# A gated linear attention followed by a multiplicative FFN: alpha of chunks 2 to 7 loaded by pairs of chunks

## The chip, the core and the metric

The kernel runs on one core of one Trainium2 chip. The metric is the device time of one execution in microseconds, smaller is better. Several executions are made of each kernel, and their median counts. One execution is taken with the hardware profiler; its span is the time between the first and the last instruction of the program, and its device time is a little longer.

## What is computed

The first part is a recurrence over 768 positions, for 4 batches and 8 heads of 48 values. Its output, read as 3,072 tokens of 384 values, goes through a feed-forward part with two gates that are multiplied.

```python
for t in range(S):
    state = alpha[:, :, t, :, None] * state + np.einsum('bhd,bhe->bhde', k[:, :, t], v[:, :, t])
    y[:, :, t] = np.einsum('bhd,bhde->bhe', q[:, :, t], state)
...
x = y.transpose(0, 2, 1, 3).reshape(B * S, H * D)
a = x @ w1
b = x @ w2
h = a * b @ w3
return h @ w_out
```

The shapes: q, k, v and alpha are 4 x 8 x 768 x 48 in float32, with alpha between 0.8 and 1; w1 and w2 are 384 x 1,024, w3 is 1,024 x 1,024, w_out is 1,024 x 384, all in float64. In DRAM the 48 values of one head at one position are 192 contiguous bytes, and the next position of the same head follows directly.

## The kernel before

**Chunks.** The positions are cut into N = 24 chunks of C = 128, six for each batch. A chunk's positions lie on the 128 partitions, its 8 heads of 48 values beside one another, 384 columns. For chunk n, `load_a` (L132) fetches alpha, `load_kq` (L138, L139) k and q, and `load_v` (L144) v. Each of these is one transfer of 192 KB in 1,024 rows of 192 bytes. All go through SP's queue, except v of chunks 3 to 7, which goes through POOL's.

**Decays.** `logs` (L272) takes the logarithm of alpha on ACT. `decays` (L287) multiplies it on TensorE with a 128 x 128 matrix of zeros and ones, `sums`, which adds up the logarithms along the positions: for even chunks with a minus sign and over the positions that come after, for odd ones over those up to and including the position itself. So two neighbouring chunks meet in a common point, between them. The exponentials of the sum and of its negative are `e` (L293, L294), and VectorE multiplies k and q with them (`decayed`, L303). Chunks below LATE = 10 do the sum as one float32 product; later ones split the logarithm in two float32r parts and do two products (L290).

**Attention in a chunk.** TensorE transposes k and q (`transposed`, L325) and ACT copies the result out (L327). `scores` (L365) multiplies keys and queries, VectorE masks (L368), `attend_state` (L385) applies the state from before, `attend` (L391) adds the chunk's own part, ACT copies it out (L395), and a store by SP (L262) writes it to `xd` in DRAM. `outer` (L337) makes the chunk's own contribution to the state, and VectorE adds it (L345, L347). At each even chunk but the first of a batch, `advance` (L354 to L356) on POOL scales the state with a decay. That decay is the product of three rows: two of exponentials (L296, L298) and the row of alpha at the chunk's first position (L279). They are written to a small tensor `ends` in DRAM by POOL's queue, and read back in another layout (L311).

**Buffers.** Alpha has three buffers (tag "ac"), k and q three, the logarithm two, v five. A transfer into a buffer waits until its last reader is done, so the load of alpha of chunk 5 waits for the logarithm of chunk 2 and for the small transfer L279 that reads chunk 2's alpha.

**Weights.** Beside the chunks, `convert` turns the float64 weights, loaded as 64-bit integers (L192, 512 KB each), into float32 by bit operations on VectorE and ACT (L200 to L210), and splits them into float32r parts (L217, L219, and by way of TensorE L233 to L235).

**Order.** The main loop, L600 to L671, runs over the chunks. In each turn n it issues the stores, alpha of chunk n + 5, k and q of n + 3 (from chunk 6 on n + 4), attention of chunks n - 1 and n, transposes of n + 1, weight conversion, the product of n + 2 with its decays, logarithms of n + 4 and sums of n + 3. Before the loop a prologue loads alpha of chunks 0 to 4. A scheduler then orders the instructions of each engine by its own estimate of when they can run; `issue_after` gives it a limit for single ones. In turn 5 `split_x` (L413 to L415) splits the first 384 tokens of x into three parts in the buffer "x3" of pool `tr[0]`, and the first gates' products begin (L421), which fill the rest of the kernel.

Of the kernel before, what the change touches and what calls it, by code (L numbers as in the profile page):

```python
# [10 lines left out]
FP32 = mybir.dt.float32  # L11
FP32R = mybir.dt.float32r
# [3 lines left out]
AF = mybir.ActivationFunctionType  # L16
# [32 lines left out]
def kernel(  # L49
# [12 lines left out]
    nc = tc.nc  # L62
    B, H, S, D = q.shape
    C = 128
    DM = H * D
    DF = moe_w1.shape[1]
    NCH = S // C
    N = B * NCH
    NP = H // 2
    DP = 64  # L70
    KM = DM // C
# [3 lines left out]
    TG = G * C  # L75
    CW = 512
    AHEAD = 4
    LATE = 10
    assert D <= DP and DM % C == 0 and DF % CW == 0 and S % C == 0 and N % G == 0
    assert DM <= 512 and TG <= 512  # L80

    def pool(name, bufs, stack=ctx, **kw):
        return stack.enter_context(tc.tile_pool(name=name, bufs=bufs, **kw))
# [4 lines left out]
    tr = [pool("tr0", 1)]  # L88
# [14 lines left out]
    def bank():  # L103
        return ps.tile([C, 512], FP32, tag="bank", name="bank")

    st, mark = {}, {}
# [10 lines left out]
    ends = {n: dram.tile([3, DM], FP32, name=f"ends{n}") for n in range(2, N, 2) if n % NCH}  # L117
# [7 lines left out]
    def rows(src, n):  # L125
        b, c = divmod(n, NCH)
        return src[b, :, ds(c * C, C), :].rearrange("h p d -> p h d")

    def load_a(n):
        if n < N:  # L130
            st["a", n] = inp.tile([C, H, D], FP32, tag="ac", name="ac")
            nc.sync.dma_start(out=st["a", n], in_=rows(alpha, n))  # L132

# [7 lines left out]
    def load_v(n):  # L141
        if n < N:
            st["v", n] = vs[n % len(vs)]
            (nc.gpsimd if 2 < n < 8 else nc.sync).dma_start(out=st["v", n][:, :, 0:D], in_=rows(v, n))  # L144

    nc.scalar.preload_act_table_set(LN_EXP_SET)
    load_a(0)
    load_kq(0)
    load_a(1)
    load_v(0)  # L150
    load_kq(1)
    load_a(2)


# [26 lines left out]
    make_identity(nc, ident)  # L181
    nc.gpsimd.tensor_copy(out=signs[:, 0], in_=ident)
    nc.gpsimd.tensor_scalar_mul(signs[:, 1], ident, -1.0)
    for x in Ts + decs:
        nc.gpsimd.memset(x, 0.0)

# [80 lines left out]
    def logs(n):  # L267
        if n >= N:
            return
        a = st.pop(("a", n)).rearrange("p h d -> p (h d)")  # L270
        la = st["la", n] = work.tile([C, DM], FP32, tag="la", name="la")
        nc.scalar.activation(la, a, AF.Ln)  # L272
        if n >= LATE:

            t = st["la", n] = work.tile([C, 2, DM], FP32R, tag="la2", name="la2", bufs=1)
            nc.scalar.copy(t[:, 0], la)
            nc.vector.tensor_sub(t[:, 1], la, t[:, 0].bitcast(FP32))
        if n in ends:
            nc.gpsimd.dma_start(out=ends[n][2:3], in_=a[0:1])  # L279

    def decays(n):
        if n >= N:
            return
        lc = bank()[:, 0:DM]
        la = st.pop(("la", n))
        if n < LATE:
            nc.tensor.matmul(lc, sums[:, n % 2].bitcast(FP32), la, start=True, stop=True)  # L287
        else:
            for i in range(2):
                nc.tensor.matmul(lc, sums[:, n % 2], la[:, i], start=(i == 0), stop=(i == 1))  # L290

        e = st["e", n] = work.tile([C, 2, DM], FP32, tag="e", name="e", bufs=3)
        nc.scalar.activation(e[:, 0], lc, AF.Exp, scale=-1.0)  # L293
        mark["e", n] = nc.scalar.activation(e[:, 1], lc, AF.Exp).ins  # L294
        if n in ends:
            mark["pool"] = nc.gpsimd.dma_start(out=ends[n][0:1], in_=e[0:1, 0]).ins  # L296
        if n + 1 in ends:
            mark["pool"] = nc.gpsimd.dma_start(out=ends[n + 1][1:2], in_=e[C - 1:C, 1]).ins  # L298
        load_ends(n)
# [6 lines left out]
    def load_ends(n):  # L306
        if n not in ends:
            return
        with nc.allow_non_contiguous_dma(reason="single values to partitions"):
            for i in range(2):  # L310
                nc.gpsimd.dma_start(out=decs[n // 2 % 2][ds(DP * i, D)].rearrange("d m j -> d (m j)"),  # L311
                                    in_=ends[n].rearrange("m (j i d) -> i d (m j)", i=2, d=D)[i])
# [95 lines left out]

    def split_x(g, i):
        x = st.pop(("xT", g))  # L410
        t = tr[i].tile([C, 3, KM, TG], FP32R, tag="x3", name="x3")
        st["x3", g] = t
        nc.scalar.activation(t[:, 0], x, AF.Copy, scale=1.0 - 2.0 ** -13)  # L413
        nc.vector.tensor_sub(t[:, 1], x, t[:, 0].bitcast(FP32))
        mark["x3"] = nc.vector.scalar_tensor_tensor(t[:, 2], t[:, 0].bitcast(FP32), -1.0 - 1.0 / P, x,  # L415
                                                    op0=ALU.mult, op1=ALU.add).ins
# [146 lines left out]
    fill = deque()  # L563
# [12 lines left out]
    for half in range(DF // CW):  # L576
        for kk in range(KM):
            weights.extend(load_gates(i, kk, half) for i in range(2))

    logs(0)  # L580
    decays(0)
    decayed(0)
    transposed(0)
    with after_marks(("e", 0)):
        logs(1)
    decays(1)
    fetch(1)
    load_a(3)
    load_kq(2)
    decayed(1)  # L590
    fetch(2)
    load_v(1)
    load_a(4)

# [5 lines left out]
    for n in range(N + 1):  # L600
# [5 lines left out]
        for m in (n + 3,) * (n <= FIRST) + (n + 4,) * (n >= FIRST):  # L606
            load_kq(m)
            if n < FIRST - 2:
                fetch(raws)
            if n >= FIRST:  # L610
                load_v(m - 1)
# [8 lines left out]
        if n - 2 in begin and n > FIRST:  # L620
            g, tiles = begin[n - 2]
            with after_marks(("ms", n), ("qkT", n + 1)):
                split_x(g, 0)
            fill.extend(gate(g, f) for f in tiles)
        pieces = (3, 3, 2, 0)[(n - FIRST) % 4] if n >= FIRST else 0
        if n == 0:
            with after_marks(("qkT", 0)):
                logs(2)
            decays(2)
            with after_marks(("e", 2)):  # L630
                logs(3)
# [29 lines left out]
        if n == FIRST - 1:  # L661
            assert len(done) == 2 * KM
            g, tiles = begin[n - 2]
            with after_marks("l"):
                split_x(g, 0)
            fill.extend(gate(g, f) for f in tiles)
# [32 lines left out]
    for i, x in enumerate(todo):  # L699
        with tc.issue_after(ends_of_part1[0]), tc.issue_after(ends_of_part1[1]):  # L700
            while order and i >= order[0][0]:
                split_x(*order.pop(0)[2:])
                if order:
                    load_x(order[0][2], nc.gpsimd)
        for _ in x:
            pass
        owed += 2.0
        with tc.issue_after(ends_of_part1[0]), tc.issue_after(ends_of_part1[1]):
            convert(int(owed), 4)
        owed -= int(owed)  # L710
        if i == halfway + 1:
            first.close()
            w3o = pool("w3op", 1, side="right", reuse_waits="tile").tile([C, 3, KF, DM], FP32R, name="w3o")
        if folded < KF:
            if w3o and folds and next(folds[0], None) is None:
                folds.popleft()
                folded += 1
        elif lastp is None:
            settle()
            folding.close()  # L720
            lastp = pool("lastp", 1, reuse_waits="tile")
            for n in range(4):
                load_ab(n)
# [40 lines left out]
```

## Time and profile before

| | |
|---|---|
| median of three runs | 477.14 us (476.88 to 477.63) |
| the profiled execution | 476.57 us |
| its span | 474.8 us |
| TensorE busy over the span | 456.5 us, 96% |
| VectorE, ACT, POOL busy | 359.1, 279.6, 76.6 us |
| alpha's loads (L132) | 24 transfers of 192 KB, median 5.2 us from issue to landing |
| logarithms (L272) | 24 of 546 ns |
| packets under 512 bytes | 99,360 of 148,783 |

How to read it: lines such as L287 are lines of the kernel before. A busy time counts an engine's instructions, not what it waits for. The rows over 40 slices of the span have one digit per slice of 11.87 us, the busy share in tenths. The chain of waits follows the work that ended last back to the start: at each step to what released it. Float32 products appear as two records each.

### The profile page before, as it was taken

The numbers are of one execution on the slowest core, as the hardware profiler recorded it, in microseconds if no ns is written. First come the engines' busy times: TensorE is split into PE (matmuls) and PEld (weight loads), VectorE is DVE, ScalarE is ACT, GpSimd is POOL, SyncE is SP. The second block draws the span as 40 slices with busy tenths as digits, with TensorE's granted clock in tenths as the row PEclk, the third lists the DMA queues.
The fourth block names the chain that finished last, engine by engine and source line by source line (L and its number), as shares of the span: only waits on it lengthen the run. The fifth ranks groups of instructions, "written<-read, shape, count | busy, mean of one in ns | idle before, by whom it ended". The sixth has DMA issues, their size and how long they took to land.

```text
span 474.8 us, 10017 instructions
## 1 busy us (share of the span) xinstructions
PE 456.5 (96%) x3836; PEld 432.7 (91%) x3836; DVE 359.1 (76%) x578; ACT 279.6 (59%) x555; POOL 76.6 (16%) x144
## 2 busy tenths in 40 slices
PE   4878899999999999999999999999999999999997
PEld 2666689899999998999999999999999999999996
DVE  2778796899979888999999868855542876666761
ACT  4668765768668563988877675654543533333330
POOL 3433122104201310121221202111011000000000
PEclk9988899999999999999999999999999999999999
DMA  9999999999899944467685532202012976555511
GB/s 179 216 209 189 228 187 247 221 239 224 184 221 206 240 142 136 137 207 251 204 271 164 182 128 84 99 35 101 33 51 88 257 233 191 163 166 174 177 51 50
DMA packets 148783, 80.29 MB, mean 169 GB/s; under 512 B 99360, under 2 KB 140576, under 8 KB 148736
## 3 DMA queue, kind: packets, MB, share of 16 engines
q1 hardware_dynamic: 142960, 64.44, 55.5%
q0 software_dynamic: 5776, 15.22, 10.2%
q8 instruction: 30, 0.49, 0.5%
q14 instruction: 17, 0.14, 0.1%
HBM read 57.58 MB, written 22.06 MB: 168 GB/s over the span
## 4 chain that ended last, share of the span: by engine, by line
PE 85%; DMA 5%; DVE 4%; ACT 2%; issue 1%; SPq 1%; POOL 1%; DVEq 0%; ACTq 0%; POOLq 0%
PE bank L421 70%; PE bank L365 4%; DMA kq<-in_q_dram 4%; PE bank L391 3%; PE bank L325 2%; PE bank L385 2%; PE bank L523 1%; PE bank L337 1%; PE bank L287 1%; DMA xT<-xd 1%; PE bank L290 1%; DVE qk L303 1%; DVE ms L368 1%; DVE x L415 1%; SPq L262 1%
## 5 line engine op out<-in xcount | busy, mean ns | idle before, releaser
L421 PE MATMUL bank<-x,w 128*128 128x384 f32 x1152 | 212.6, 338 | 1.1 <-DVE x L415 0.6
L421 PEld LDWEIGHTS bank<-x,w 128*128 128x128 f32 x1152 | 200.2, 188 | 4.0 <-PE bank L421 0.9
L421 PE MATMUL bank<-w3o,ab 128*128 128x384 f32 x576 | 100.2, 336 | 0.0
L421 PEld LDWEIGHTS bank<-w3o,ab 128*128 128x128 f32 x576 | 99.9, 188 | 0.0
L446 ACT ACTIVATE bank<-bank 128x384 f32<-128x384 f32 x96 | 45.7, 476 | 41.2 <-PE bank L421 40.6
L430 ACT ACTIVATE t<-bank 128x384 f32<-128x384 f32 x64 | 31.5, 494 | 57.4 <-PE bank L421 56.2
L496 POOL DMA_DIRECT2D abd<-ab x45 | 26.3, 583 | 144.9 <-DVE ab L482 126.2
L482 DVE TENSOR_TENSOR ab<-bank,r 128x384 f32<-128x384 f32 x44 | 24.4, 554 | 24.9 <-ACT bank L446 15.9
L552 DVE TENSOR_TENSOR ab<-abl,ab 128x1024 fp32r<-128x1024 f32 x24 | 29.4, 1224 | 12.3 <-ACT ab L551 12.3
L327 ACT COPY qkT<-bank 128x512 f32<-128x512 f32 x48 | 25.8, 590 | 20.5 <-PE bank L325 20.5
L551 ACT ACTIVATE ab<-abl 128x1024 fp32r<-128x1024 f32 x24 | 25.4, 1060 | 20.2 <-PE bank L421 18.3
L421 PE MATMUL bank<-wo,w3T 128*128 128x384 f32 x192 | 35.9, 334 | 0.0
L303 DVE TENSOR_TENSOR qk<-kq,e 128x768 f32<-128x768 f32 x24 | 22.9, 954 | 14.9 <-ACT e L294 8.3
L421 PEld LDWEIGHTS bank<-wo,w3T 128*128 128x128 f32 x192 | 33.5, 188 | 0.0
L368 DVE TENSOR_TENSOR ms<-bank,keep 128x512 int32<-128x512 int32 x48 | 31.2, 683 | 0.1
L432 DVE SCALAR_TENSOR_TENSOR o<-bank,t 128x384 f32<-128x384 f32 x24 | 13.4, 557 | 23.0 <-issue 13.7
L432 DVE SCALAR_TENSOR_TENSOR r<-bank,t 128x384 f32<-128x384 f32 x40 | 22.1, 554 | 11.4 <-ACT t L430 8.5
L205 ACT ACTIVATE power<-power,rebias 128x512 uint32<-128x512 uint32 (+1 forms) x36 | 25.1, 699 | 9.2 <-DVE power L204 9.0
L365 PEld LDWEIGHTS bank<-qkT 48*128 48x128 f32 x384 | 24.4, 193 | 6.3 <-issue 3.0
L365 PE MATMUL bank<-qkT 48*128 48x128 f32 x384 | 29.3, 291 | 0.4 <-ACT x L395 0.4
L553 DVE SCALAR_TENSOR_TENSOR ab<-ab,abl 128x1024 fp32r<-128x1024 f32 x24 | 29.2, 1218 | 0.0
L391 PE MATMUL bank<-ms,v 128*64 128x128 f32 x384 | 27.6, 289 | 0.0
(81 smaller groups left out, 578.9 us busy)
## 6 DMA issues: line engine op xcount, KB each, us to landing
raw<-in_moe_w_dram SPq DMA_DIRECT2D x28, 512.0 KB, 5.2
abl<-abd SPq DMA_DIRECT2D x24, 512.0 KB, 4.4
abd<-ab POOLq DMA_DIRECT2D x45, 192.0 KB, 2.8
xT<-xd POOLq DMA_DIRECT2D x9, 576.0 KB, 4.5
ac<-in_alpha_dram SPq DMA_DIRECT2D x24, 192.0 KB, 5.2
kq<-in_k_dram SPq DMA_DIRECT2D x24, 192.0 KB, 5.7
kq<-in_q_dram SPq DMA_DIRECT2D x24, 192.0 KB, 5.7
xd<-x SPq DMA_DIRECT2D x48, 96.0 KB, 4.0
```

The costliest lines, as they stand in the source:

```text
L303: mark["qk", n] = nc.vector.tensor_mul(qks[n % 3][:, :, :, 0:D], st.pop(("kq", n)), st.pop(("e", n)).rearrange("p i (h d) -> p i h d", h=H ...
L327: mark["qkT", n] = nc.scalar.copy(qkT[:, :, :, ds(DP * half, DP)], tp[half]).ins
L365: nc.tensor.matmul(sc[i][:, j, :], qkT[r, 0, j, :], qkT[r, 1, j, :], start=True, stop=True)
L368: masked = nc.vector.tensor_tensor(ms[:, i].bitcast(I32), sc[i].bitcast(I32), keep_bc, op=ALU.bitwise_and)
L391: nc.tensor.matmul(to, vc[:, 2 * j + i, :], ms[:, i, j, :], start=(n % NCH == 0 and j % HP == 0), stop=(j % HP == HP - 1), skip_group_chec ...
L421: nc.tensor.matmul(p, w[part][i], x[part][i], start=start and part == parts[0] and i == 0, stop=stop and part == parts[-1] and i == n - 1, ...
L430: nc.scalar.activation(t, p1, AF.Copy, scale=(1.0 + 1.0 / P) * scale)
L432: nc.vector.scalar_tensor_tensor(to, p2, scale, t, op0=ALU.mult, op1=ALU.add)
L446: nc.scalar.activation(p, p, AF.Copy, scale=1.0 + 1.0 / P)
L496: (nc.gpsimd if late else nc.sync).dma_start(out=abd[g][:, f, :], in_=ab)
L552: nc.vector.tensor_sub(t[:, 1], ab, t[:, 0].bitcast(FP32))
L553: nc.vector.scalar_tensor_tensor(t[:, 2], t[:, 0].bitcast(FP32), -1.0 - 1.0 / P, ab, op0=ALU.mult, op1=ALU.add)
```

## The change

Alpha of chunks 2 to 7 is loaded as three pairs, (2, 3), (4, 5) and (6, 7). A pair's 256 positions go onto 128 partitions by twos: partition p holds positions 2p and 2p + 1, for each head 96 values that are contiguous in DRAM, 384 bytes. The first chunk of a pair thus lies on partitions 0 to 63 and the second on 64 to 127. One logarithm over 768 columns, in place, serves a pair. The sums of a chunk become two float32 products that accumulate, one with the even positions of the pair and one with the odd ones, each with a matrix that takes the chunk's positions from its half of the partitions and puts the sums out in order (`sums2`, four 128 x 128 matrices, made on POOL at the start). The pairs and the matrices lie in the memory of the first "x3" buffer, which is free until the first `split_x`; there are two buffers for three pairs, so the pair (6, 7) takes the place of (2, 3). The rows of alpha for `ends` of chunks 2 and 4 are copied from DRAM to DRAM instead of out of the loaded tile. The prologue loads the pair (2, 3) where it loaded chunk 2 and the pair (4, 5) where it loaded chunk 4; turn 1 of the loop loads (6, 7) where it loaded chunk 6; the loads of chunks 3, 5 and 7 fall away.

```diff
+    PAIRED = 8
...
+    def paired(n):
+        return 2 <= n < PAIRED
+
     def load_a(n):
-        if n < N:
+        if paired(n):
+            if n % 2 == 0:
+                b, c = divmod(n, NCH)
+                x = pairs[n // 2 % 2]
+                nc.sync.dma_start(out=x.rearrange("p h s d -> p h (s d)"), in_=alpha[b, :, ds(c * C, 2 * C), :].rearrange("h (p s) d -> p h (s d)", s=2))
+                st["a", n] = st["a", n + 1] = x
+        elif n < N:
             st["a", n] = inp.tile([C, H, D], FP32, tag="ac", name="ac")
             nc.sync.dma_start(out=st["a", n], in_=rows(alpha, n))
...
+    spare = tr[0].tile([C, 3 * KM * TG], FP32R, tag="x3", name="x3")[:].bitcast(FP32)
+    sums2 = spare[:, 0:4 * C].rearrange("p (e s t) -> p e s t", e=2, s=2)
+    pairs = [spare[:, ds(4 * C + i * 2 * DM, 2 * DM)].rearrange("p (h s d) -> p h s d", h=H, s=2) for i in range(2)]
...
+    for e, val in ((0, -1.0), (1, 1.0)):
+        nc.gpsimd.memset(sums2[ds(e * C // 2, C // 2), e], val)
+        nc.gpsimd.memset(sums2[ds((1 - e) * C // 2, C // 2), e], 0.0)
+        nc.gpsimd.affine_select(out=sums2[:, e], in_=sums2[:, e], fill=0.0, base=e * C,
+                                compare_op=mybir.AluOpType.is_ge if e else mybir.AluOpType.is_gt,
+                                pattern=[[-1, 2], [1, C]] if e else [[1, 2], [-1, C]],
+                                channel_multiplier=-2 if e else 2)
     for x in Ts + decs:
         nc.gpsimd.memset(x, 0.0)
...
     def logs(n):
         if n >= N:
             return
-        a = st.pop(("a", n)).rearrange("p h d -> p (h d)")
+        a = st.pop(("a", n))
+        if paired(n):
+            if n % 2 == 0:
+                nc.scalar.activation(a, a, AF.Ln)
+                st["la", n] = st["la", n + 1] = a
+                b, c = divmod(n, NCH)
+                if n in ends:
+                    nc.gpsimd.dma_start(out=ends[n][2:3].rearrange("m (h d) -> m h d", h=H), in_=alpha[b:b + 1, :, c * C, :])
+            return
+        a = a.rearrange("p h d -> p (h d)")
...
         la = st.pop(("la", n))
-        if n < LATE:
+        if paired(n):
+            for i in range(2):
+                nc.tensor.matmul(lc.rearrange("p (h d) -> p h d", h=H), sums2[:, n % 2, i], la[:, :, i, :],
+                                 start=(i == 0), stop=(i == 1))
+        elif n < LATE:
             nc.tensor.matmul(lc, sums[:, n % 2].bitcast(FP32), la, start=True, stop=True)
...
     def split_x(g, i):
         x = st.pop(("xT", g))
-        t = tr[i].tile([C, 3, KM, TG], FP32R, tag="x3", name="x3")
+        t = tr[i].tile([C, 3 * KM * TG], FP32R, tag="x3", name="x3").rearrange("p (s k t) -> p s k t", s=3, k=KM)
```

## The prediction

> **What bounds the kernel now.** I read the page's forty slices first, to see where TensorE is not the limit.
>
> ```profile
> PE   4878899999999999999999999999999999999997
> PEclk9988899999999999999999999999999999999999
> DMA  9999999999899944467685532202012976555511
> ```
>
> One slice is 11.87 us. From slice six on TensorE is full, and the stretches answer from 60.45 to 474 us gives 410.49 busy of 413.55. The change touches chunks 2 to 7, all in the first five slices, so its worth is the shift of the moment at which TensorE becomes full. Before that the DMA engines are full too. So I read the chain of waits for the first 60 us.
>
> ```profile
> 13.68 1.35 PE bank L287 x2
> ...
> 18.17 4.77 DMA kq<-in_q_dram
> ...
> 24.91 6.25 DMA kq<-in_q_dram
> ...
> 47.43 6.22 DMA kq<-in_q_dram
> ...
> 59.03 1.28 DVE x L415
> 60.31 0.14 issue
> 60.45 2.34 PE bank L421 x12
> ```
>
> The columns are start, length, what. Three loads of q carry 17 us of it: up to 31.16 us the chain is loads that arrive one after the other; from 31.16 to 45 it runs through DVE and ACT (weight conversion, masks, exponentials); then the load for chunk 7 and the split of x. How much room TensorE has there, the stretches answer shows (busy us of PE, PEld, DVE, ACT, POOL; granted clock; DMA share; GB/s):
>
> ```profile
> 12.56:47.71 35.15, 28.88 (x390) 22.15 (x389) 27.90 (x49) 24.95 (x54) 12.96 (x22) 0.90 1.11 205
> 31.00:39.00 8.00, 6.81 (x60) 5.54 (x56) 7.45 (x14) 4.96 (x12) 2.48 (x4) 0.57 1.02 189
> 2.00:7.60 5.60, 1.62 (x2) 0.50 (x2) 1.25 (x3) 1.94 (x5) 2.23 (x10) 1.00 1.33 196
> ```
>
> TensorE idles 35.15 - 28.88 = 6.27 us between the transposes of chunks 1 and 6 (L325 at 12.56 and 47.71). These idle times are its waits for loads and for what follows from them; VectorE waits 6.5 us in five multiplications (L303) for q:
>
> ```profile
> PE bank L325 <- DVE qk L303: 3.7, 3, 1.9
> PE bank L325 <- DVE T L347: 1.2, 1, 1.2
> PE bank L337 <- DMA v<-in_v_dram: 0.9, 1, 0.9
> PE bank L287 <- ACT la L272: 0.8, 1, 0.8
> DVE qk L303 <- DMA kq<-in_q_dram: 6.5, 5, 2.2
> ```
>
> [...] From 2.00 to 7.60 us the trace holds 192-byte packets alone, 5,809 of them: 5.60 us x 16 / 5,809 = 15.4 ns. [...] The trace has a clock of 0.57 from 31 to 39 us, after the idle stretch before 32.53, and an L287 product takes 1.35 us at 13.68 but 0.65 at 62.78.
>
> **The change part by part.**
>
> *Alpha's loads.* Six loads of 192 KB in 1,024 rows of 192 B become three of 384 KB in 1,024 rows of 384 B. One old load takes 64 packets per engine x 15.4 ns = 0.99 us. For 384 B no row of the trace stands. Bounds: if bytes set the price, nothing is saved; if packets do, 0.49 us per chunk, 3.0 in all. [...] I take that estimate: 0.29 us per chunk, 1.7 in all.
>
> *What moves on SP's queue.* SP issues in order[...]. Before, L132 for chunks 4 and 5 sits from 13.78 for 3.50 us, as chunk 5's buffer waits until the small transfer out of chunk 2's (L279, issued at 11.53) has landed; k and q of chunk 3 stand behind it, and the DMA moves only 113 GB/s from 21 to 22 us, some 0.5 us lost. In the changed order chunk 3's alpha comes with 2, 5 with 4, 7 with 6; the pairs have own buffers, that wait is gone. The new wait: the load of 6 and 7 needs the buffer of 2 and 3, free after chunk 3's sums on TensorE; k, q and the raw weights queue behind it. I expect these sums done by 17.4 us (below) and the load at about 20, so it costs nothing. Beyond 18.5 to 20 it would. q of chunk 3 then lands at 22.94 - 4 x 0.29 - 0.5 = 21.3, q of chunk 4, with chunk 7's alpha 0.70 earlier in the line, at 31.16 - 1.7 - 0.5 + 0.7 = 29.6: about 1.5 us early.
>
> *The sums.* Each of six chunks gets a second fp32 product: 0.65 us at full clock, 1.3 at half. Chunk 2's starts at 13.6, where the half clock ends after one product: +0.65; chunks 3, 4, 5 and 7 +0.65 each; chunk 6's (38.18) falls at the edge of the half clock, +1.0. Sum 4.25 us, bounds 3.9 and 7.8. It has 6.27 us of idle to lie in, so at most 2.0 us of earlier arrival can be used by this engine. Step by step: chunk 2's +0.65 is given back where chunk 3 no longer waits 0.77 for its logarithm (16.40): chunk 3's sums end at 17.4, scores (L365) of chunk 1 start at 17.4 against 17.24. Chunk 4's lies before the wait of 1.12 at 24.14. Chunk 5's lies before L385, which waited already for POOL's state (L356, done 28.50), then L325 of chunk 4 waited 1.19 at 32.53. That state comes from chunk 2's exponential, 0.65 later, so at 29.1; L385 and L365 then end at 30.9 instead of 32.53: this agrees with 29.6 for q plus 0.96 for L303. So 1.5 us is won at 31. From 32.53 to 45.83 TensorE has no gap: chunk 6's and 7's +1.65 leave it at 45.98 instead of 45.83 even with the 1.5, still ahead of 47.71 - 1.5 by 0.2 us. There the cover ends: TensorE is late next. The strided moving operand (runs of 48 in 96) has no row; I take nothing for it; the upper bound, a doubled read in all twelve products, would be 7.8 us more.
>
> *Logarithms.* Six of 0.54 become three over 768 columns. From L272 (0.55 for 384) and L413 (1.17 for 1,152) 0.81 ns per column, so 0.86: ACT saves 0.66 us. The first now needs 384 KB landed: about 0.4 later than 11.40, ended at 12.8, before chunk 2's sums at 13.6. The pair 4, 5 ends at 20.5 against 20.32; w L217 and qkT L327 queue behind, 0.2 us, hidden before L325's wait at 24.14. At 40.28 chunk 7's logarithm leaves the chain: -0.41. But the exponential ahead of it waits for chunk 6's sums: 39.18 - 1.5 + 1.0 = 38.7 instead of 39.38. With the logarithm gone, w L217 starts at 39.6 instead of 40.55. So of 1.5 us about 1.0 is left, and VectorE (L219, L368), ACT L395, the store, the load for chunk 7 and the split of x follow it to 60.45.
>
> *POOL.* Four memsets (0.28 each, as L185) and two selections over 256 columns (0.28 for 128, so 0.5): 2.1 us after 3.6, ending at 6.4; POOL was idle from 4.22 to 11.53. The first product waits for sums (L173), issued ahead of them, so not for these. Rows 0 of alpha go from DRAM to DRAM: waits of 7.30 and 3.67 us go, but the next (L311, 20.64) still waits for the exponential's row to land. Nothing won. The split of x takes the pairs' memory over: it waits for chunk 7's sums, 44 us, against its 55.22: free.
>
> Sum: the profiled execution took 476.57 us (span 474.8); -1.0 makes 475.6. The three runs have a median of 477.14, 0.57 above it; on that scale 476.1.
>
> **The rivals.**
>
> *TensorE takes the bound* (slower). Place: 12.56 to 47.71. If the half clock holds over most of the added products, they cost 7.8 us against 6.27 idle: +1.5, and no load is used; with gaps that cannot be used, up to +2.5. It decides from about 5.3 us of added time. For it: 28.88 busy of 35.15, no gap from 32.53 on, and a half clock twice. Against: most gaps lie just behind the new products. 478.9.
>
> *The longer rows save nothing* (it doesn't do what it says): bytes set the price. Chunk 7's alpha still comes earlier, 0.99 at q of chunk 4, less 0.5 of SP's gap, and TensorE's added products give back nothing: +0.5, 477.6. [...]
>
> *Fuller TensorE, full clock.* With fewer gaps the clock may not fall at 31 us; half clock there lasted about 6.9 us, 3.4 us of work. VectorE (27.90 busy) is late next: -2.5, 474.6. Against: before 31 its gaps stay.
>
> **How the numbers follow.** No change is within 0.2%, 0.95 us, about what a measurement of this kernel can tell. Forecast 0.50, own range -2.2 to -0.3 (474.9 to 476.8): faster 0.35, same 0.15. TensorE 0.22, all slower. No saving 0.17: 0.10 same, 0.07 slower. Full clock 0.11, faster. Together 0.46, 0.25, 0.29. For 8 in 10 the range goes from 474.6, the full clock's value, to 479.0, most of TensorE's case.
>
> **What would show it.** Right: q of chunks 3 and 4 landing near 21.3 and 29.6, L303's waits for q under 5 us, SP without its 3.5 us stand, TensorE's idle from the first to the second of those transposes near 1 to 2 us, L421's run of twelve starting near 59.5. Wrong: a rate in alpha's loads as before; TensorE waiting less and still starting that run at 60.5 or later; SP standing at the load of 6 and 7; more time at half clock.

## The result, and the profile after

| | before | after |
|---|---|---|
| median | 477.26 us (20 runs, 476.09 to 478.86) | 475.75 us (20 runs, 473.91 to 478.06) |
| ratio | | 0.9967, 95% interval 0.9955 to 0.9980 |
| the profiled execution | 476.57 us | 475.50 us |
| its span | 474.8 us | 473.8 us |
| mean granted clock of TensorE | 0.989 | 0.996 |
| packets under 512 bytes | 99,360 | 96,240 |

The changed kernel is 1.5 us faster, a third of a per cent; the forecast was 1.0 us. The same three rows of the page's forty slices, for the kernel after:

```profile
PE   4988899999999999999999999999999999999996
PEclk9999999999999999999999999999999999999999
DMA  9999999999999934567685532212013986555511
```

The second row has lost its three eights: each of these slices now has 90% of the full clock or more. The stretches of the kernel after (busy us of PE, PEld, DVE, ACT, POOL with their instructions; granted clock; DMA share; GB/s) show it more finely; those of the kernel before that the prediction does not show come first:

```profile
48.00:57.00 9.00, 8.27 (x115) 6.10 (x111) 6.62 (x12) 6.86 (x14) 0.66 (x2) 0.81 1.17 249
57.00:61.00 4.00, 2.83 (x11) 1.86 (x12) 4.00 (x6) 3.22 (x8) 1.92 (x3) 1.00 0.73 179
```

and of the kernel after:

```profile
12.50:31.00 18.50, 17.72 (x220) 12.23 (x220) 14.86 (x28) 12.83 (x28) 5.78 (x11) 1.00 1.16 228
31.00:39.00 8.00, 7.09 (x107) 5.40 (x104) 6.93 (x12) 6.44 (x15) 3.15 (x5) 1.00 1.10 246
39.00:48.00 9.00, 7.85 (x120) 5.96 (x116) 6.40 (x12) 5.54 (x13) 3.47 (x7) 1.00 0.94 203
48.00:57.00 9.00, 7.68 (x93) 5.15 (x89) 8.22 (x13) 8.04 (x19) 2.33 (x4) 1.00 0.91 213
57.00:61.00 4.00, 3.62 (x11) 3.14 (x12) 2.55 (x5) 2.08 (x6) 0.07 (x1) 0.57 1.02 210
```

From 31 to 39 us the DMA now moves 246 GB/s against 189, and TensorE runs at 1.00 against 0.57; its 7.09 us of busy time hold 107 matmul records where 6.81 us held 60. From 48 to 57 us it is 1.00 against 0.81. The half clock has not vanished, though. It stands at the end of the table, 0.57 over the 4 us in which the first gates begin, with 0.50 in every part of them between 57.5 and 60.5 us; the kernel before had 1.00 there.

VectorE's waits in the first 62 us of the kernel after (us in total, times, longest):

```profile
DVE qk L337 <- ACT e L328: 8.1, 2, 4.4
DVE w L240 <- ACT w L238: 3.7, 6, 0.7
DVE qk L337 <- DMA kq<-in_q_dram: 1.6, 2, 1.2
```

L337 is the multiplication that was L303. It waits 1.6 us for q where it waited 6.5; the split of a weight (L240, before L219) in turn waits 3.7 us for ACT where it waited 1.5. From 12.5 to 57 us VectorE is busy for 36.41 us, against 34.81 before: 1.6 us more of its work is done. The loads of q land at these times (us), each the start of its issue on SP plus the time to its landing:

| q of chunk | before | after |
|---|---|---|
| 3 | 22.94 | 21.77 |
| 4 | 31.16 | 30.92 |
| 5 | 38.80 | 36.51 |
| 6 | 46.51 | 44.11 |
| 7 | 53.65 | 48.28 |

For chunk 4 these are the lines on the two loads, issued at 24.91 before and at 24.20 after:

```profile
DMA to landing us min/median/max: 6.3/6.3/6.3
DMA to landing us min/median/max: 6.7/6.7/6.7
```

All five come earlier, but that of chunk 4 by 0.24 us alone. The chain of waits of the kernel after (start, length, what):

```profile
24.20 5.21 DMA kq<-in_q_dram
29.41 0.51 POOL T L390
29.98 0.24 issue
30.22 0.68 DVE mant L228
30.97 0.45 issue
31.42 0.95 DVE qk L337
32.37 0.61 DVE mant L231
...
55.99 1.28 DVE x L448
57.31 1.30 PE bank L455 x3
58.67 3.32 PE bank L455 x12
61.99 0.32 PE bank L321
```

The chain breaks the load of q of chunk 4 off at 29.41, which is not its landing: its sixteen parts report from 29.12 to 30.92, VectorE needs all of them, and POOL's scaling of the state (L390) does not use q. What VectorE does meanwhile differs. Before, it had nothing left and stood 2.13 us until q was there; the addition of POOL's state and the conversion came behind the multiplication. After, it waits 0.67 us for POOL's state, which comes later (29.41 to 29.92, before 27.99 to 28.50), does the addition and two instructions of weight conversion, and comes to the multiplication at 31.42, 0.17 later than before. But that other work is now out of the way. The next split of a weight (L240) runs at 33.67 against 35.10, with one mask fewer ahead of it; where both kernels have done the same work, ahead of the next L222 (L201 before), it is 35.48 against 36.31, 0.83 us. Then q of chunk 5 has landed 2.29 us earlier: its L337 starts at 36.60 against 38.89. The split of x (L448) starts at 55.99 in the chain, against 57.76.

The last two lines take part of that back: the twelve products start at 58.67 against 60.45, and last 3.32 us, with a granted clock of 0.68 over them, against 2.34. The sums behind them start at 61.99 against 62.78: 0.8 us of the 1.8 is left. The spans differ by 1.0.

### The profile page after: what moved, and what is told of

Same layout as the page of the kernel before. It is cut to its first block, busy times and chain, and to the rows that moved or that the text cites. A ratio compares the mean times of both kernels' runs of the same rounds, so it can differ in the third digit from the quotient of the medians.

```text
span 473.8 us, 10043 instructions
## 1 busy us (share of the span) xinstructions
PE 458.9 (97%) x3848; PEld 433.5 (92%) x3848; DVE 359.0 (76%) x578; ACT 279.4 (59%) x552; POOL 79.8 (17%) x150
## 2 busy tenths in 40 slices
DMA packets 145663, 80.29 MB, mean 169 GB/s; under 512 B 96240, under 2 KB 137456, under 8 KB 145616
## 4 chain that ended last, share of the span: by engine, by line
PE 87%; DMA 4%; DVE 3%; SPq 3%; issue 1%; ACT 1%; POOL 0%; DVEq 0%
PE bank L455 72%; PE bank L399 4%; PE bank L425 4%; DMA kq<-in_q_dram 3%; PE bank L419 2%; PE bank L359 2%; PE bank L557 1%; DMA x<-in_alpha_dram 1%; PE bank L371 1%; PE bank L324 1%; SPq L213 1%; DVE ms L402 1%; SPq L149 1%; DVE qk L337 1%; SPq L148 1%
## 5 line engine op out<-in xcount | busy, mean ns | idle before, releaser
L361 ACT COPY qkT<-bank 128x512 f32<-128x512 f32 x48 | 25.8, 589 | 21.3 <-PE bank L359 21.3
L585 ACT ACTIVATE ab<-abl 128x1024 fp32r<-128x1024 f32 x24 | 25.5, 1061 | 21.3 <-PE bank L455 18.0
L337 DVE TENSOR_TENSOR qk<-kq,e 128x768 f32<-128x768 f32 x24 | 22.9, 953 | 10.2 <-ACT e L328 8.3
L425 PE MATMUL bank<-ms,v 128*64 128x128 f32 x384 | 26.3, 279 | 0.0
```

The lines of the kernel that those rows point to most:

```text
L337: mark["qk", n] = nc.vector.tensor_mul(qks[n % 3][:, :, :, 0:D], st.pop(("kq", n)), st.pop(("e", n)).rearrange("p i (h d) -> p i h d", h=H ...
L361: mark["qkT", n] = nc.scalar.copy(qkT[:, :, :, ds(DP * half, DP)], tp[half]).ins
L425: nc.tensor.matmul(to, vc[:, 2 * j + i, :], ms[:, i, j, :], start=(n % NCH == 0 and j % HP == 0), stop=(j % HP == HP - 1), skip_group_chec ...
```

## The experiments

Every ratio is to the kernel before, run on the same chip, and comes from medians. The profiled execution of a kernel can lie over 2 us from its median, so the profiles are read for places, the ratios for sizes. One thing can be read from all profiles alike: the start of the last product of the sums (166 to 171 us; 173 and 176 with extra loads), and the time from there to the end of the span. That remainder is 307.2 to 307.5 us in before, after and every experiment but the last. So whatever these executions win or lose, they do before that point.

### Rows of 192 bytes in the changed kernel

Only the transfers change: a pair comes by two of them, in the old rows.

```diff
-                nc.sync.dma_start(out=x.rearrange("p h s d -> p h (s d)"), in_=alpha[b, :, ds(c * C, 2 * C), :].rearrange("h (p s) d -> p h (s d)", s=2))
+                for i in range(2):
+                    nc.sync.dma_start(out=x[:, :, i, :], in_=alpha[b, :, ds(c * C, 2 * C), :].rearrange("h (p s) d -> p h s d", s=2)[:, :, i, :])
```

> The changed kernel with each pair fetched by two transfers of 192-byte rows, one for the even and one for the odd positions: packets as before the change, all else as after it, in the same order on every engine but SP. Theory A (the longer rows move the loads of k and q forward, and that is the gain): the 1.7 us of DMA work come back, so most of the gain goes: 0.999 to 1.001 of the kernel before, VectorE waiting 4 us or more for q. Theory B (the gain comes from TensorE's added products: a clock that doesn't fall, and the other order that the scheduler gives VectorE): stays at 0.996 to 0.998, full clock from 31 to 39 us.

Measured: 1.0025 (1.0016 to 1.0034), a little above what either theory expected. Everything but the row length and the number of transfers is as in the changed kernel, and this kernel is slower than before. VectorE's wait for q, in its profile, the slowest of its executions (L338 is the multiplication):

```profile
DVE qk L338 <- DMA kq<-in_q_dram: 4.5, 3, 2.0
```

It is 4.5 us where the changed kernel has 1.6. q of chunks 3 to 7 lands at 24.01, 31.70, 39.21, 47.66 and 52.63, from 0.8 to 4.4 us later than in the changed kernel, and the twelve products start at 62.22. From 0.9967 to 1.0025 are 0.58%, 2.8 us. The short rows of a pair are not quite the old ones, since one transfer takes every second position; but the two transfers of the first pair land 1.08 us apart, as neighbours in the kernel before do (0.9 to 1.2).

Two transfers instead of one could be the cause too. So a second kernel has two transfers per pair, of four heads each, in rows of 384 bytes:

```diff
-                nc.sync.dma_start(out=x.rearrange("p h s d -> p h (s d)"), in_=alpha[b, :, ds(c * C, 2 * C), :].rearrange("h (p s) d -> p h (s d)", s=2))
+                for h in range(0, H, H // 2):
+                    nc.sync.dma_start(out=x[:, h:h + H // 2].rearrange("p h s d -> p h (s d)"), in_=alpha[b, h:h + H // 2, ds(c * C, 2 * C), :].rearrange("h (p s) d -> p h (s d)", s=2))
```

> The changed kernel with each pair fetched by two transfers of four heads each, still in rows of 384 bytes: the number of transfers of the run with short rows, the rows of the change, the same order on every engine but SP. If the length of the rows is what that run lost: as the change, 0.996 to 0.998 of the kernel before. If three more transfers in a queue[...] were what it lost: 1.000 to 1.0025.

Measured: 0.9978 (0.9968 to 0.9988), which overlaps the changed kernel's interval. By the medians the row length makes 0.47%, 2.2 us, of the difference, with an uncertainty of 0.13%; the number of transfers 0.11%, which the noise covers.

### The price of a row

Extra loads of alpha at the very start of the kernel before, ahead of all other loads: four of 384 KB in rows of 384 bytes in one kernel, eight of 192 KB in rows of 192 bytes in the other. Nothing reads them.

```diff
+    for i in range(4):
+        nc.sync.dma_start(out=probe[:, ds(i * 2 * DM, 2 * DM)].rearrange("p (h d) -> p h d", h=H), in_=alpha[3, :, ds(i * C, 2 * C), :].rearrange("h (p s) d -> p h (s d)", s=2))
...
+    for i in range(8):
+        nc.sync.dma_start(out=probe[:, ds(i * DM, DM)].rearrange("p (h d) -> p h d", h=H), in_=rows(alpha, 18 + i % 6))
```

> The kernel before with four more loads ahead of all others, each 384 KB of alpha in 1,024 rows of 384 bytes, into memory that nothing reads: the price of such rows by itself. If a row has one price whatever its length (15.4 ns per engine), the four take 4 x 0.99 = 4.0 us and run at about 390 GB/s. [...] If it follows bytes, 7.9 us and 196 GB/s.

> The kernel before with eight more loads ahead of all others, each 192 KB of alpha in 1,024 rows of 192 bytes, the same bytes as the four long ones: 8 x 0.99 = 7.9 us at 196 GB/s under every theory.

The stretches of the kernel with long rows (the last number is GB/s; at 4.50 the extra loads run, at 9.50 the usual ones in short rows):

```profile
4.50:7.00 2.50, 0.00 (x0) 0.00 (x0) 0.00 (x0) 0.00 (x0) 0.00 (x0) 1.00 1.27 261
9.50:12.00 2.50, 1.31 (x2) 0.50 (x2) 0.00 (x0) 0.52 (x1) 0.00 (x0) 1.00 1.45 186
```

and of the kernel with short rows:

```profile
4.50:7.00 2.50, 0.00 (x0) 0.00 (x0) 0.00 (x0) 0.00 (x0) 0.00 (x0) 1.00 1.24 191
9.50:12.00 2.50, 0.00 (x0) 0.00 (x0) 0.00 (x0) 0.00 (x0) 0.00 (x0) 1.00 1.45 187
```

One engine of sixteen moves 261 / 16 = 16.3 bytes per ns in long rows and, with 186.5 as the mean of the two later stretches, 186.5 / 16 = 11.7 in short ones. A row of 384 bytes takes 23.5 ns, two of 192 take 2 x 16.47 = 32.9: a ratio of 0.715. With the 191 GB/s of the extra loads themselves it is 0.73. The landings say the same: the long loads land about 1.52 us apart (5.90, 7.39, 8.94), the short ones 1.05 (4.97 to 11.27), so 384 KB take 1.52 against 2.10 us, a ratio of 0.72, or 0.29 us saved for each chunk. The two kernels took 482.72 and 485.19 us in one execution each, 0.31 us for each of eight chunks, but single executions of one kernel differ by more than this.

So neither bytes alone nor packets alone set the price: by bytes a row of 384 would take 32.9 ns, by packets 16.5, and it takes 23.5. The prediction's saving of 0.29 us for each chunk is met. It was its author's estimate, between the bounds of nothing and 0.49 us, and the trace of the kernel before has no such row; of its 0.99 us for a load it leaves 0.70, a ratio of 0.71. The price of a short row is 16.5 ns here, where the prediction had 15.4 from the packets between 2.00 and 7.60 us. What a price is made of, two row lengths do not show. As an estimate, a fixed 9.4 ns for a row and 7.0 ns for each 192 bytes give the two measured prices; other splits may.

### The second product alone, left out, and a third

Three kernels change the number of products of the sums in chunks 2 to 7. In the kernel before a product with a matrix of zeros is added:

```diff
-            nc.tensor.matmul(lc, sums[:, n % 2].bitcast(FP32), la, start=True, stop=True)
+            nc.tensor.matmul(lc, sums[:, n % 2].bitcast(FP32), la, start=True, stop=not 2 <= n < 8)
+            if 2 <= n < 8:
+                nc.tensor.matmul(lc, zero, la, start=False, stop=True)
```

> The kernel before with a second product for the sums of chunks 2 to 7, with a matrix of zeros: TensorE's cost of the change alone, no change in loads, logarithms or POOL's copies. Theory A: 4.25 us more on TensorE and no earlier load: 1.001 to 1.004. Theory B: full clock from 31 to 39 us and VectorE's order of the changed kernel bring the gain without any change of loads: 0.996 to 0.999.

In the changed kernel the second product is left out, so the odd positions of chunks 2 to 7 do not enter the sums:

```diff
-            for i in range(2):
-                nc.tensor.matmul(lc.rearrange("p (h d) -> p h d", h=H), sums2[:, n % 2, i], la[:, :, i, :],
-                                 start=(i == 0), stop=(i == 1))
+            nc.tensor.matmul(lc.rearrange("p (h d) -> p h d", h=H), sums2[:, n % 2, 0], la[:, :, 0, :],
+                             start=True, stop=True)
```

> The changed kernel without the second product of each sum (it leaves out the odd positions of chunks 2 to 7): the loads of the change without TensorE's added cost. Theory A: TensorE freed of 4.25 us, so the whole 1.5 us of earlier loads and more is kept: 0.994 to 0.9965. Theory B: gaps on TensorE return, the clock falls to half again at about 30 us, and the gain goes in part: 0.998 to 1.000.

And in the changed kernel a third one is added, with zeros:

```diff
-                                 start=(i == 0), stop=(i == 1))
+                                 start=(i == 0), stop=False)
+            nc.tensor.matmul(lc.rearrange("p (h d) -> p h d", h=H), zero, la[:, :, 0, :], start=False, stop=True)
```

> The changed kernel with a third product, by a matrix of zeros, for each sum of chunks 2 to 7: the suspected cost once more, some 4 us on TensorE. If TensorE's idle time was used up by the change (my forecast's step: 0.2 us of cover left): nearly all of it shows, 1.002 to 1.005. If it still has room: 0.997 to 0.999.

| sums | short rows | long rows |
|---|---|---|
| one product | 1 (before) | 0.9940 (0.9922 to 0.9958) |
| two | 1.0062 (1.0042 to 1.0082), 1.0025 with the pairs' logarithms, buffers and order | 0.9967 (0.9955 to 0.9980) |
| three | | 1.0083 (1.0066 to 1.0099) |

With long rows the second product costs 0.27%, 1.3 us, with an interval from 0.2 to 2.3 us; the third costs 1.16%, 5.5 us (4.5 to 6.5), for about as much work, and more than was expected of it. By the medians the first extra product lies mostly in idle time, the next does not any more. The stretch of the kernel with three products shows TensorE without idle time, where the changed kernel still had 0.78 us:

```profile
12.50:31.00 18.50, 18.50 (x203) 12.82 (x200) 14.27 (x26) 11.80 (x23) 5.15 (x10) 1.00 1.11 226
```

That fits the cover of the prediction and its end. It is not the whole of the 5.5 us: further on TensorE waits 2.9 us in one piece for the split of a weight, and that part was not taken apart.

In the kernel before the same product costs 0.62% or 3.0 us, above both expectations, although that kernel waits longer for q. There it is not the product's time alone: the order of the work changed with it, and TensorE waits at its sums for VectorE's masks, which it does not in the kernel before:

```profile
PE bank L290 <- DVE ms L373: 3.8, 2, 3.1
```

With the added product the clock is different, too. This is the stretch from 31 to 39 us of the kernel before with the added product (columns as above; before: clock 0.57, 189 GB/s):

```profile
31.00:39.00 8.00, 6.88 (x96) 4.93 (x88) 5.82 (x11) 5.66 (x14) 2.74 (x5) 1.00 1.12 241
```

The clock is full and the DMA moves 241 GB/s, both as in the changed kernel, and yet this kernel is slower than before. The kernel with short rows has 1.00 there as well, and is slower too. The kernel with one product also has 1.00 there, with TensorE busy for 6.21 us, less than the 6.81 of the kernel before. So what brings the full clock at 31 us is not shown, and it is not enough to make a kernel faster.

The kernel with one product starts the twelve products earlier and at full clock (its chain):

```profile
56.62 2.34 PE bank L454 x12
58.95 0.65 PE bank L320 x2
```

Its sums of chunk 9 start at 58.95, the changed kernel's at 61.99: 3.0 us. In the profiled executions none of it is left at the last sums (166.5 against 166.3). But this execution of the kernel with one product is the slowest of its six, 2.3 us above their median, so the 1.3 us of the medians are the size to go by. TensorE's waits from 60 to 170 us in it name one place where such a lead is lost; the changed kernel has no line there:

```profile
PE bank L358 <- ACT x L428: 1.6, 1, 1.6
```

### The rows for the decay from DRAM to DRAM

The kernel before with this part of the change alone:

```diff
-            nc.gpsimd.dma_start(out=ends[n][2:3], in_=a[0:1])
+            if n < 8:
+                b, c = divmod(n, NCH)
+                nc.gpsimd.dma_start(out=ends[n][2:3].rearrange("m (h d) -> m h d", h=H), in_=alpha[b:b + 1, :, c * C, :])
+            else:
+                nc.gpsimd.dma_start(out=ends[n][2:3], in_=a[0:1])
```

> The kernel before with the rows of alpha for the ends of chunks 2 and 4 copied from DRAM to DRAM: only SP's stand of 3.5 us at chunk 5's alpha goes. Theory A with the 0.5 us that I gave this stand: 0.998 to 0.9995. Theory B: no change, 0.9995 to 1.0005, with the half clock from 31 us on as before.

Measured: 1.0001 (0.9987 to 1.0015). SP's queue in the timeline of this kernel (start, length with the waits in it):

```profile
13.91 3.84 SPq L132 DMA_DIRECT2D ac<-in_alpha_dram  x2
17.85 0.72 SPq L138 DMA_DIRECT2D kq<-in_k_dram  x1
```

and of the changed kernel:

```profile
13.46 0.58 SPq L138 DMA_DIRECT2D x<-in_alpha_dram  x1
14.16 2.91 SPq L148 DMA_DIRECT2D kq<-in_k_dram  x1
17.11 0.90 SPq L149 DMA_DIRECT2D kq<-in_q_dram  x1
```

This run does not show that the stand is worth nothing. It shows something else: without the transfer out of chunk 2's alpha, SP stands as long as before, 3.84 us against 3.50. SP's waits in the kernel before give this transfer a small part of the stand:

```profile
SPq L132 <- DMA ends<-ac: 0.7, 1, 0.7
```

So it was not what SP mainly waited for. In the changed kernel the stand moved to the next instruction, k of chunk 3, and is 2.91 us long. What the three have in common is their end. They end at 17.28, 17.75 and 17.07, and each time the 512 KB of raw weights that were issued three transfers earlier land 0.25 to 0.28 us later (17.54, 18.03, 17.32). What links the two no run tests.

### Both chunks' products side by side

Each product of a pair needs only the 64 partitions of its chunk: the other half of its matrix is zeros. Two kernels give each chunk's product its 64 partitions alone, so that the two chunks' products may run at the same time, into two banks. The first moves the second chunk's exponentials up with them, the second leaves those where they were.

```diff
+                for e in range(2):
+                    r = ds(e * C // 2, C // 2)
+                    nc.tensor.matmul(both[e].rearrange("p (h d) -> p h d", h=H), sums2[r, e, i], la[r, :, i, :],
+                                     start=(i == 0), stop=(i == 1))
```

> The changed kernel with the four products of a pair issued together, each over the 64 partitions that hold its chunk's positions, so that the two chunks use different rows of the array; the exponentials of both chunks follow at once. If such float32 products run beside one another as L365's do (16 records in 1.09 us), TensorE's added cost goes: 0.994 to 0.9955 of the kernel before. If they run one after the other, no better than the change, and the earlier exponentials cost ACT's order something: 0.9965 to 0.999.

> The same, but the exponentials of the second chunk stay where they were, so its sums hold a PSUM bank for one turn of the loop. If the products overlap and the bank is not missed: 0.994 to 0.9955. If the bank is missed, products wait for it: 0.996 to 1.000.

Measured: 0.9997 (0.9984 to 1.0010) and 0.9989 (0.9976 to 1.0001): a miss. The gain of the change is gone in the first, and most or all of it in the second. The products did what they should. In the timeline of the changed kernel the four records of one chunk take

```profile
17.21 1.56 PE L318 MATMUL bank<-x 128*128 128x384 f32 x4
```

and in that of the first of these kernels the eight records of a pair

```profile
21.39 1.56 PE L321 MATMUL bank<-x 64*128 64x384 f32 x8 [0.30 <-ACT x L294]
```

the same time. But VectorE waits for q as it did before the change, 7.2 us here and 7.6 in the second kernel, and two stretches of the first have the half clock again:

```profile
31.00:39.00 8.00, 8.00 (x82) 6.73 (x77) 6.12 (x11) 6.96 (x15) 4.23 (x6) 0.61 1.08 243
48.00:57.00 9.00, 9.00 (x104) 7.31 (x100) 7.73 (x15) 7.42 (x17) 0.96 (x2) 0.65 1.02 232
```

To see whether the clock is the reason, the second kernel got back the two products at the odd chunk, as fillers whose result nobody reads:

```diff
+            nc.tensor.matmul(bank()[:, 0:DM], sums[:, 0].bitcast(FP32), spare[:, 0:DM], start=True, stop=True)
+            nc.tensor.matmul(bank()[:, 0:DM], sums[:, 0].bitcast(FP32), spare[:, 0:DM], start=True, stop=True)
```

> The changed kernel with the products of a pair beside one another on two halves of the array, as in the run before that held the second chunk's sums in PSUM, and two products of constants that nothing reads where the second chunk's products stood: TensorE is as full as in the changed kernel. If the half clock from 30 to 38 and from 47 to 54 us ate that run's gain: full clock there, and 0.995 to 0.9975. If something else ate it (the order, the bank held longer): 0.998 to 1.001 whatever the clock.

Measured: 1.0055 (1.0036 to 1.0074). The clock is 1.00 from 31 to 39 us, 0.87 and 0.94 in the two stretches behind, and the kernel is the slowest of the three, slower than either theory expected. VectorE's wait for q in it:

```profile
DVE qk L350 <- DMA kq<-in_q_dram: 4.9, 4, 2.0
```

It waits 4.9 us for q again, with the same long rows. q of chunk 3 lands 1.3 us later than in the changed kernel, which accounts for part of it, but q of chunks 4 to 6 lands earlier (30.19, 35.53 and 43.90; there 30.92, 36.51 and 44.11). So early loads are not enough either; it matters what other work VectorE has until they land. Which of the moved instructions brings the waits back was not taken apart, nor whether a bank is missed; TensorE waits for VectorE's masks by 2.8 and 3.6 us in one piece in the two kernels without fillers. Shown is only that a fuller clock by fillers does not bring the gain back.

### A filler ahead of the first gates

What remains is the half clock from 57 us on. In the changed kernel TensorE stands 0.93 us for the split of x between the first three products of the gates and the rest. There two products that nobody reads are put:

```diff
+            if part == 0 and warm:
+                t, filler = warm.pop(), bank()
+                for cols in (TG, 2 * C):
+                    nc.tensor.matmul(filler[:, 0:cols], sums[:, 0].bitcast(FP32), t[:, 0, 0, 0:cols].bitcast(FP32),
+                                     start=True, stop=True)
```

> The changed kernel with two float32 products whose result nobody reads, of 384 and 256 columns, put behind the first three products of the first gates, where TensorE stood 0.93 us for the split of x. In the changed kernel the granted clock is 0.57 from 57 to 61 us and the first gates' twelve products take 3.32 us, against 2.34 before; in the kernel with one product for the sums it kept full clock there. If that late half clock is part of what the second products cost at the end, the twelve products take 2.34 us here, the next sums start near 61.1 instead of 61.99, and the ratio to before is 0.0015 to 0.002 under the changed kernel's 0.9967: 0.9947 to 0.9952. Rival: the clock at the run's start is worth nothing, as in the earlier filled kernel, or falls all the same: 0.9967, or 0.997 for the 0.15 us by which the filler delays the run.

Measured: 1.0307 (1.0285 to 1.0329), far from both expectations. At the place itself the first holds. TensorE in the timeline of this kernel:

```profile
54.90 0.79 PE L459 MATMUL bank<-x,w 128*128 128x384 f32 x3 [0.25 <-ACT x L449]
55.52 1.24 PE L464 MATMUL bank<-x,sums 128*128 128x384 f32 x4
56.62 0.80 PE L459 MATMUL bank<-x,w 128*128 128x384 f32 x3
57.98 2.34 PE L459 MATMUL bank<-x,w 128*128 128x384 f32 x12 [0.56 <-DVE x L451]
60.15 0.81 PE L321 MATMUL bank<-la,sums 128*128 128x384 f32 x2
```

The twelve products take 2.34 us instead of 3.32, and the granted clock over 57 to 61 us is 1.00 instead of 0.57. From the first three products to the sums it is 60.15 - 54.90 = 5.25 us; in the changed kernel, where that is 55.59 to 61.83, 6.24. So the half clock there costs 1.0 us. But of the lead at 60 us only 0.5 is left at the last sums (165.8 against 166.3), and from there to the end it takes 323 us, not 307. The stretches of this kernel at that place, columns as above,

```profile
205.00:245.00 40.00, 40.00 (x226) 39.68 (x226) 17.81 (x27) 23.08 (x46) 8.85 (x15) 1.00 0.34 107
245.00:275.00 30.00, 17.94 (x93) 17.00 (x92) 26.96 (x60) 20.60 (x43) 2.72 (x4) 0.77 0.50 161
```

and of the changed kernel:

```profile
205.00:245.00 40.00, 40.00 (x229) 40.00 (x228) 39.68 (x75) 34.40 (x70) 9.82 (x15) 1.00 0.71 225
245.00:275.00 30.00, 30.00 (x181) 29.93 (x180) 28.38 (x52) 21.29 (x42) 4.78 (x8) 1.00 0.57 180
```

VectorE is 39.68 us busy from 205 to 245 us in the changed kernel, with the conversion of the last weights, and 17.81 here. From 197.6 to 244.1 us no raw weights are loaded, where the changed kernel issues eleven loads; SP waits for VectorE, 46.1 us in one piece:

```profile
SPq L213 <- DVE mant L222: 55.1, 4, 46.1
```

So that conversion comes later, and TensorE idles 12.06 us of the next 30, waiting for it. The edit adds two instructions at 55 us, and the order of the work is another 150 us later. This run answers for the clock at its place, and not for what the kernel could gain from it.

## Why the prediction was right, and where its terms were off

The forecast, the changed kernel somewhat faster because longer rows bring the loads of q earlier, is what happened: -1.5 us where -1.0 was said. That the longer rows are the cause is shown by the kernels with short rows and with two transfers. How close the number came owes something to luck: the loads were worth more than was said, and the products may have cost more, and the two partly cancel.

**Alpha's loads.** The price of a long row, the author's estimate, was met: 0.72 of two short ones, 0.29 us per chunk. Their worth was put too low. The prediction let 1.5 us arrive at 31 us, after SP's share and the earlier place of chunk 7's alpha; long rows alone gave 2.2 to 2.8 us at the end, and loads, logarithms and order together 2.8 (the kernel with one product). The transfers' saving itself is 6 x 0.29 = 1.7 us, within what the noise allows for the 2.2.

**q of chunks 3 and 4.** This step failed. q of chunk 3 was put at 21.3 and landed at 21.77, 1.2 us early; q of chunk 4 was put at 29.6 and landed at 30.92, 0.24 us early where 1.5 was said. The gain is there all the same, but by another way: VectorE did other work up to the multiplication instead of standing 2.13 us, 0.83 us ahead at 35.48, and the loads that come much earlier are those of chunks 5 to 7, by 2.3 to 5.4 us. The prediction put numbers on q only as far as chunk 4.

**SP's queue.** Wrong. The prediction held that SP stood 3.5 us for the transfer out of chunk 2's alpha and would not stand any more. That transfer was 0.7 us of it. With the transfer gone, the stand is still there in one kernel (3.84), and moved to k in the other (2.91); k of chunk 4 then stands 3.33 us, from 20.82, where it stood 2.49. What SP waits for stays open. The 0.5 us laid on this stand did not come, which is part of why q of chunk 4 is late against the forecast.

**The sums.** Their own size was not far off: the twelve products of chunks 2 to 7 take 10.55 us by the timeline, the six before 5.86, so 4.7 more, where 4.25 was said. Chunk 2's two took 2.81 us, where chunk 3's two took 1.56, so chunk 3's sums were done at 18.77 and not by 17.4; the load of chunks 6 and 7 was still issued at 20.14, as said. The transposes of chunks 1 and 6 stand at 12.83 and 46.26 in the trace after, 33.43 us apart with 30.59 busy, so TensorE idles 2.84 us, where 1 to 2 were said and 6.27 were there before. That little cover is left is what the third product points to. What the second products leave at the end may be the mis-sized term. The prediction took 0.5 us of the 1.5 for them, by way of chunk 6's exponential, and 1.0 was left; the exponential came as said (38.36 against 38.7), and so did the conversion behind it (39.79 against 39.6). Measured is 1.3 us, but the interval from 0.2 to 2.3 does not exclude 0.5. One thing at that place the prediction did not have: the half clock over the first gates (0.68 over the twelve products), 0.98 us longer for them, which the kernel with one product does not have. It was named only as a sign of failure ("more time at half clock"), with no place. How much of it is left at the end no run shows.

**Logarithms and POOL.** A pair's logarithm takes 845 ns (median of three), 0.86 us was said, and waits 0.3 us for its load in all. It was sized right. POOL's state for chunk 2 was done at 29.92, where 29.1 was said, 0.8 us late; chunk 2's sums had taken 2.81 us where some 2.1 were said.

**The start of the gates.** "Near 59.5" became 58.67, but with the clock at 0.68 over the twelve products, so that 61.99 stands against 62.78 where the sums begin: 0.8 us earlier, with 1.0 predicted.

**The rivals.** That longer rows save nothing is refuted by the pair with short rows (1.0025) and by their price. That TensorE takes the bound did not come true: the second products cost 1.3 us by the medians, less than the loads bring. The full clock at 31 us came (1.00 from 31 to 39 us), against the prediction's argument, and is not enough for the gain: the kernel before with the added product has it and loses 0.62%.

## What to carry to other kernels

Where many short rows come from DRAM, measure the row and not the byte: doubling 192 bytes to 384 saved 27 to 29% of the transfer time here, and a few extra products on an engine that waits for those loads were a fair price, up to the idle time that it had. Work out that idle time first: one more product of the same size cost 1.16% where the first had cost 0.27%. When a chain of waits ends a load early, look up when the load has landed as a whole. And before an experiment with an added instruction is read by its time, find a point behind it from which both traces take equally long to the end; where they do not, something else has changed as well.

## What was not expected of the hardware

Two float32 products, each over its own 64 partitions, ran side by side, into two banks: eight records of 64 x 384 took 1.56 us, as four of 128 x 384 do.

The half clock came back within a stretch in which TensorE was not long idle. In the changed kernel, gaps of 0.23, 0.25 and 0.93 us between 54.6 and 57.3 us were followed by a clock of 0.57 over 57 to 61 us. With the 0.93 us filled and a gap of 0.56 behind the filler, it stayed at 1.00. The length of one gap did not decide here: in the kernel with one product TensorE stood 1.74 us up to 52.24 and 0.47 us up to 56.62, and the clock stayed at 1.00 from 48 to 61 us. What decides is open.
